# A transformer block in float32: the second half of the tokens is stored by token tiles, two feed-forward blocks change their form, and some transfers are moved

## The chip, the core and the metric

The kernel runs on one core of one Trainium2 chip. A core has five engines that run their own instruction lists side by side: TensorE (PE in the profile; its weight loads are listed apart as PEld) multiplies matrices and writes to PSUM, VectorE (DVE) and ScalarE (ACT) work on tiles in PSUM and SBUF, GpSimd (POOL) works on tiles in SBUF, and SyncE (SP) issues nearly all transfers of this kernel. Transfers (DMA) run on 16 DMA engines. Each engine takes its instructions in the order in which they were written; an instruction that has to wait holds back all that stand behind it on its engine. The metric is the device time in microseconds, from one execution of the whole program; lower is better.

## The reference

One transformer block on 2048 tokens of width 640, all in float32:

```python
q, k, v = qkv[0], qkv[1], qkv[2]                # 32 heads of width 20
scores = jnp.einsum("bhqd,bhkd->bhqk", q, k) * (Dh ** -0.5)
o = jnp.einsum("bhqk,bhkd->bhqd", softmax(scores), v)
h = x + o.transpose(0, 2, 1, 3).reshape(B, S, D) @ wo      # qkv = layernorm(x) @ wqkv
g = silu(layernorm(h) @ w_gate)                 # 640 -> 1728
h2 = h + (g * (layernorm(h) @ w_up)) @ w_down   # 1728 -> 640
```

## The kernel before

**Precision.** Each float32 operand of a product is split into a rounded part "hi" and a remainder "lo" (helper `split`: ACT writes hi, DVE or POOL writes lo, lines L78 and L79), and three matmuls take the place of one (hi·hi, lo·hi, hi·lo).

**The stages.** First come the q, k, v products (up to about 340 us), then attention (to about 1560 us), where each of 32 units is four heads by 512 queries, then the output product and the second layernorm, then the feed-forward part. While attention runs, `prepare_weights` splits the feed-forward weights on POOL, one task in most slots of the loop, and stores them in DRAM: `w_d` for gate and up, `d_d` (one block of rows, plain) and `j_d` (two blocks together) for down.

**The feed-forward part.** The 1728 hidden columns are 14 blocks of 128 (`f` = 0 to 13, the last one half wide). The 2048 tokens are four chunks of 512, taken in two pairs: chunks 0 and 1 ("pair 0"), then chunks 2 and 3 ("pair 1"). The list `ELEMENTS` is pair 0 with f = 13, 0, 1, ..., 12 and then pair 1 with the same, 28 elements `e`. An element's gate and up products for both chunks are done by `blocks` with a scheme of sums that needs 54 matmuls of 512 columns instead of 60; it reads the chunks' normalized, transposed activations `z2_c` and sums of them, `t14` and `t32`, as moving operand, in 8 steps (`products`, L1038, into the four PSUM banks `ps_a`). The weights come through `unit_ring`, `last_ring` (SP issues the loads, L824).

**The down products** follow one step at a time, in between, from the list `waiting` (`next_down`; how many per step says the table `RATES`). Two blocks f, f+1 are normally done together: seven steps for 256 tokens, each of three matmuls of 320 columns (`seven`, L1123, four banks `ps_b`), whose operand `yp` needs sums and splits on POOL and ACT (`prepare`, L1113 to L1116 and L78, L79), and whose results go partly to `h` and partly to sums of their own (`own`), which are added to `h` at the end on POOL (L1161). A block done alone ("plain": before, f = 12 and 13 of pair 0 and f = 10 to 13 of pair 1) takes four steps for 256 tokens and adds to `h` directly on DVE (L1128). The down weights come through `down_ring`, nine places of the tile `halves`.

**The late tokens.** SBUF holds one pair at a time. So during the first elements of pair 0 the chunks 2 and 3 are normalized, transposed on PE (L1374, five matmuls per tile of 128 tokens, two `ps_a` banks), copied by ACT to `zz` (L1379), split to a staging tile `kept` (L78, L79; two buffers), and written to DRAM (`z_d`); POOL forms the sums of the two chunks (L1391), which are split and written as well (`t_d`). The rows of `h` themselves are written too (`h_d`). This work is a list `late` of which one item runs at the end of each step, four items per tile of 128 tokens of both chunks, 17 in all. The writes are put on SP's list one item after the split (`store`, L1347). Down products of two blocks together can only begin when this list is empty, since their tiles `yp` and `own` take its place.

**The swap.** At the end of pair 0 the new activations and sums are loaded over the old ones (`swap`, L1420, at the steps in `SWAPS`), and `h` of chunks 2 and 3 comes back (`bring_back`).

## Time and profile before

| what | value |
|---|---|
| three timed runs, median | 2158.71 us |
| lowest, highest | 2153.14, 2159.97 us |
| the profiled execution's own time | 2154.66 us |
| its span, first to last instruction | 2152.9 us |
| PE busy in the span | 2092.1 us (97%) |
| DVE, ACT, POOL busy | 1739.1, 1302.5, 729.0 us |
| moved by DMA | 294.28 MB, 137 GB/s over the span |

A page of the profile gives busy times by engine, the span in 40 slices, the transfers, the chain of work that ended last, and the costliest groups of instructions. Rows of a timeline are: start in us, duration in us, engine and source line, operation, output<-input, shapes, how many were merged (x), and in brackets how long the engine was idle before and what ended that. "PEclk" is the granted TensorE clock as a share of full speed. The span of a row of merged matmuls reaches a little past the start of the next row, because matmuls overlap; the pitch from one row's start to the next row's start is what they cost. In a stage table the numbers behind an engine are its busy time and its count of instructions.

### The profile page before, as it was taken

The page shows a single profiled execution, that of the slowest core. Times are in us where ns is not written, and L with a number is a line of the kernel's source. Part 1 is how long each engine was busy: PE and PEld are TensorE (multiplying, and loading weights), DVE is VectorE, ACT ScalarE, POOL GpSimd, SP SyncE. Part 2 cuts the span into 40 slices and gives each one's busy share as a digit, 9 for nine tenths or more (in the row PEclk, how much of TensorE's full clock was granted, in tenths as well). Part 3 has the DMA queues.
Part 4 walks back from the last instruction along what each step waited for, and adds up shares of the span by engine and source line. Part 5 has one row for each costly group of instructions (what it writes and reads, how often), then busy time and mean ns, then how long its engine had stood idle before and what let it go on. Part 6 is the DMA issues. An engine that isn't in the chain of part 4 may idle for free.

```text
span 2152.9 us, 35419 instructions
## 1 busy us (share of the span) xinstructions
PE 2092.1 (97%) x12594; PEld 1213.1 (56%) x12594; DVE 1739.1 (81%) x2885; ACT 1302.5 (60%) x2587; POOL 729.0 (34%) x1037
## 2 busy tenths in 40 slices
PE   7999999999999999999999999999996999999999
PEld 5766775333333333333333333345685788788888
DVE  6999997999999999999999999974373566566667
ACT  4322217999989999999999999976632222112221
POOL 5222212343342433443300001011155544565447
PEclk9999999999999999999999999999998999999999
DMA  7665533342524434435412122211259446785452
GB/s 239 180 180 168 155 106 93 113 147 78 169 89 146 129 119 125 158 107 156 142 47 63 48 68 54 73 59 52 64 178 284 146 156 201 284 283 168 162 184 96
DMA packets 213833, 294.28 MB, mean 137 GB/s; under 512 B 46792, under 2 KB 99016, under 8 KB 213656
## 3 DMA queue, kind: packets, MB, share of 16 engines
q1 hardware_dynamic: 200072, 265.79, 39.0%
q10 hardware_dynamic: 13584, 26.23, 4.0%
q8 instruction: 100, 1.64, 0.3%
q14 instruction: 77, 0.63, 0.1%
HBM read 196.77 MB, written 94.37 MB: 135 GB/s over the span
## 4 chain that ended last, share of the span: by engine, by line
PE 85%; DMA 5%; DVE 4%; POOL 3%; ACT 1%; issue 1%; SPq 0%; ACTq 0%; POOLq 0%; DVEq 0%
PE acc L878 23%; PE ps_max L179 15%; PE ps_one L868 14%; PE ps_a L1038 13%; PE ps_b L1123 7%; PE ps_one L420 5%; DVE mx L173 3%; PE ps_wide L169 2%; PE ps_one L454 2%; PE ps_max L611 2%; DMA z_d<-kept 1%; DMA halves<-j_d 1%; PE ps_b L611 1%; DMA t_d<-kept 1%; DMA o_t<-o_d 1%
## 5 line engine op out<-in xcount | busy, mean ns | idle before, releaser
L874 ACT ACTIVATE probs<-ps_one 128x512 f32<-128x512 f32 x2048 | 1045.0, 623 | 134.8 <-PE ps_one L868 130.0
L185 DVE TENSOR_REDUCE mx<-ps_max 128x1 f32<-128x512 f32 x1632 | 1021.0, 683 | 95.5 <-PE ps_max L179 50.5
L868 PE MATMUL ps_one<-q_stk,k_stk 62*128 62x512 f32 x2048 | 550.5, 421 | 3.9 <-ACT probs L874 3.2
L878 PE MATMUL acc<-probs,v_stk 128*32 128x512 f32 x4096 | 546.3, 605 | 0.3
L179 PE MATMUL ps_max<-k_stk,q_stk 60*128 60x512 f32 x1632 | 541.1, 459 | 2.4 <-DVE mx L185 1.5
L179 PEld LDWEIGHTS ps_max<-k_stk,q_stk 60*128 60x128 f32 x1632 | 230.3, 184 | 428.5 <-DVE mx L185 412.5
L868 PEld LDWEIGHTS ps_one<-q_stk,k_stk 62*128 62x128 f32 x2048 | 299.8, 185 | 84.1 <-ACT probs L874 55.1
L173 DVE TENSOR_REDUCE mx<-ps_wide 128x2 f32<-128x1024 f32 x208 | 240.7, 1217 | 14.5 <-PE ps_wide L169 14.1
L1240 DVE TENSOR_TENSOR tmp<-ps_a,tmp 128x512 f32<-128x512 f32 x208 | 141.3, 690 | 136.0 <-PE ps_a L1038 108.7
L1123 PE MATMUL ps_b<-halves,yp 128*128 128x320 f32 x1116 | 197.5, 312 | 15.2 <-ACT yp L78 5.6
L1123 PEld LDWEIGHTS ps_b<-halves,yp 128*128 128x128 f32 x1116 | 180.1, 190 | 35.3 <-issue 7.1
L878 PEld LDWEIGHTS acc<-probs,v_stk 128*32 128x32 f32 x4096 | 80.8, 108 | 159.9 <-issue 151.5
L1038 PE MATMUL ps_a<-t,units 128*128 128x512 f32 x624 | 167.1, 405 | 0.1
L196 POOL CAST both<-neg 128x16 fp32r<-128x16 f32 x32 | 6.6, 206 | 467.3 <-DVE neg L192 228.3
L1038 PE MATMUL ps_a<-z,units 128*128 128x512 f32 x516 | 135.5, 398 | 0.0
L79 POOL TENSOR_TENSOR yp<-y,yp 128x256 fp32r<-128x256 f32 x104 | 65.0, 625 | 198.2 <-ACT yp L78 198.1
L1038 PEld LDWEIGHTS ps_a<-t,units 128*128 128x128 f32 x624 | 115.7, 193 | 20.5 <-DVE kept L79 1.0
L1128 DVE TENSOR_TENSOR h<-ps_b,h 128x320 f32<-128x320 f32 x228 | 103.4, 482 | 8.0 <-PE ps_b L1123 7.0
L1285 ACT ACTIVATE tmp<-tmp 128x512 f32<-128x512 f32 x26 | 16.4, 632 | 147.7 <-DVE tmp L1240 147.6
L1038 PEld LDWEIGHTS ps_a<-z,units 128*128 128x128 f32 x516 | 94.5, 190 | 16.8 <-ACT tmp L1254 0.5
L78 ACT ACTIVATE yp<-tmp 128x512 fp32r<-128x512 f32 x44 | 27.8, 632 | 121.3 <-POOL tmp L1116 121.3
L1038 PE MATMUL ps_a<-z,lasts 128*128 128x512 f32 x324 | 92.7, 394 | 0.7 <-DMA z<-z_d 0.7
(155 smaller groups left out, 2061.6 us busy)
## 6 DMA issues: line engine op xcount, KB each, us to landing
units<-w_d SPq DMA_DIRECT2D x186, 256.0 KB
w_d<-stage SPq DMA_DIRECT2D x106, 256.0 KB
halves<-j_d SPq DMA_DIRECT2D x77, 320.0 KB
j_d<-stage SPq DMA_DIRECT2D x42, 320.0 KB
raw<-qk_d SPq DMA_DIRECT2D x70, 160.0 KB
k_stk<-qk_d SPq DMA_DIRECT2D x64, 160.0 KB
q_stk<-qk_d SPq DMA_DIRECT2D x64, 160.0 KB
rb<-r_d SPq DMA_DIRECT2D x32, 256.0 KB
```

Of the source, the lines that this page charges most:

```text
L79: lo_engine.tensor_tensor(out=lo, in0=src, in1=hi.bitcast(F32), op=ALU.subtract)
L173: nc.vector.tensor_reduce(mx[:, :, pair, t, kc], ps, axis=AX.X, op=ALU.max)
L179: nc.tensor.matmul(ps, queries[u][rows, pair, t * P : (t + 1) * P], keys[u // NC][rows, pair, kc * CH : (kc + 1) * CH], start=True, stop=True,
L185: nc.vector.tensor_reduce(mxs[u][:, b, pair, t, kc : kc + 1], ps, axis=AX.X, op=ALU.max)
L420: nc.tensor.matmul(ps, w[:, k, m * P : (m + 1) * P], a[:, k, :], start=(n == 0 and k == 0), stop=(n == 2 and k == ND - 1),)
L868: nc.tensor.matmul(ps, keys[u // NC][rows, p, kt * P : (kt + 1) * P], queries[u][rows, p, :], start=True, stop=True,)
L874: nc.scalar.activation(probs[p][:, b, :], ps, AF.Exp, scale=scale)
L878: nc.tensor.matmul(acc[32 * j : 32 * j + 32, :], values[u // NC][:, kt, j * VW : j * VW + 32], probs[j // 2][:, j % 2, :], start=(kt == 0) ...
L1038: nc.tensor.matmul(ps, w[k][:, i], z[k][:, j], start=(first and m == 0), stop=(last and m == len(n) - 1),)
L1123: nc.tensor.matmul(ps, a, b, start=(n == 0), stop=(n == len(pairs) - 1))
L1128: nc.vector.tensor_tensor(out=h, in0=ps, in1=h, op=ALU.add)
L1240: add = lambda out, ps, x: nc.vector.tensor_tensor(out=out, in0=ps, in1=x, op=ALU.add)
```

## The change

1. **Layout.** `z_d` and `z2_c`, and `t_d`, `t14`, `t32`, are stored by token tile and part: for each quarter of the columns, first the token tile t, then hi or lo, then the two column blocks, then 128 tokens. A write of one token tile now puts 512 numbers (2 KB) in a row, where it put 128 (512 bytes). The moving operand of an `L1038` product (L1057 now) is now four stretches of 128 numbers, 512 numbers apart, where it was 512 in a row. The loads of the swap take one stretch of a partition instead of two.
2. **Staging.** Three tiles instead of two hold a 512-column split until it is written: one of its own, and two that lie over places 6 to 9 of `halves`, which has ten places now instead of nine. As long as the list of late items isn't empty, `down_ring` issues six loads only.
3. **More, smaller late items.** Six per tile of 128 tokens instead of four (a `store` between the two transposes, the two splits of the sums apart; the lo part of the second goes to DVE): 26 instead of 17, so that the list ends in element 4 at step 4 instead of element 3 at step 3. `h` of chunk 2 is written before, in the loop of the last output products.
4. **Two blocks plain.** f = 0 and 1 of pair 0 are done alone: their y is split when it is formed, and their down products need neither `yp` nor `own`, so that they run while the late items do (`RATES` are raised to 10 to 14 for the elements 1 to 6). `prepare_weights` gets a load and four pieces of weights more (7 tasks).
5. **The swap** loads the sums T2, T1, T3 and T4 in elements 14 and 15, where T2 and T1 were loaded in element 13. Also, in the last attention units, the rows of x for `h` are loaded one slot later, behind the second load of `o_t`.

SP's list at the first late writes. `kept` and `halves` are staging tiles; the shape at the end of a row is how many stretches, then what is in one. Before:

```order
L1347 DMA h_d<-h_19637 128x640
L1347 DMA z_d_63<-kept_20182 256x1x128
L1347 DMA z_d_63<-kept_20185 256x4x128
L824 DMA units<-w_d_68 128x512
L1347 DMA h_d<-h_19636 128x640
L1347 DMA z_d_64<-kept_20217 256x1x128
L1347 DMA z_d_64<-kept_20220 256x4x128
L824 DMA units<-w_d_68 128x512
L824 DMA units<-w_d_69 128x512
L1347 DMA t_d_65<-kept_20265 1024x1x128
```

Now:

```order
L1380 DMA z_d_63<-kept_20224 128x256
L1380 DMA z_d_63<-kept 128x2x512
L843 DMA units<-w_d_68 128x512
L843 DMA units<-w_d_69 128x512
L1380 DMA z_d_64<-kept_20286 128x256
L1380 DMA z_d_64<-halves 128x2x512
L843 DMA lasts<-w_d_70 128x512
L843 DMA units<-w_d_69 128x512
L1380 DMA t_d_65<-halves 256x1x512
L843 DMA units<-w_d_69 128x512
L1380 DMA t_d_66<-kept 256x1x512
```

The writes have longer stretches, one `h_d` write per tile is gone, and more unit loads stand between them.

PE's list from the second transpose of the second token tile (chunk 3) to the next one (chunk 2, third tile). `z`, `t` with `units` or `lasts` are the gate and up products, `halves,y` are down products. Before:

```order
L1374 MATMUL ps_a<-ident,z_20285 128x128 x5
L1038 MATMUL ps_a<-t_19639,units 128x512 x6
L1123 MATMUL ps_b<-halves,y 128x320 x2
L1038 MATMUL ps_a<-z_0_3040,units 128x512 x6
L1038 MATMUL ps_a<-z_0_3040,lasts 128x512 x3
L1123 MATMUL ps_b<-halves,y 128x320 x2
L1038 MATMUL ps_a<-t_19638,units 128x512 x6
L1123 MATMUL ps_b<-halves,y 128x320 x4
L1374 MATMUL ps_a<-ident,z_20319 128x128 x5
```

Now:

```order
L1421 MATMUL ps_a<-ident,z_20372 128x128 x5
L1057 MATMUL ps_a<-t_19656,units 128x512 x6
L1057 MATMUL ps_a<-z_0_3042,lasts 128x512 x3
L1151 MATMUL ps_b<-halves,y 128x320 x6
L1057 MATMUL ps_a<-z_1_3043,units 128x512 x6
L1057 MATMUL ps_a<-z_1_3043,lasts 128x512 x3
L1151 MATMUL ps_b<-halves,y 128x320 x3
L1057 MATMUL ps_a<-z_1_3043,lasts 128x512 x3
L1151 MATMUL ps_b<-halves,y 128x320 x6
L1057 MATMUL ps_a<-z_0_3042,units 128x512 x6
L1151 MATMUL ps_b<-halves,y 128x320 x3
L1421 MATMUL ps_a<-ident,z_20425 128x128 x5
```

Four steps instead of three lie between the two transposes, with 27 matmuls of 512 columns instead of 21 and 18 of 320 columns instead of 8.

SP's list at the swap, from the first load of a new activation on. Before:

```order
L1420 DMA z_0_3040<-z_d_63 128x2x1024
L824 DMA units<-w_d_80 128x512
L1420 DMA t_19639<-t_d_66 128x2x1024
L824 DMA units<-w_d_67 128x512
L824 DMA halves<-j_d_90 128x640
L1420 DMA z_0_3040<-z_d_63 128x2x1024
L824 DMA units<-w_d_67 128x512
L824 DMA halves<-j_d_90 128x640 x2
L1420 DMA t_19638<-t_d_65 128x2x1024
```

Now:

```order
L1468 DMA z_0_3042<-z_d_63 128x2048
L843 DMA units<-w_d_80 128x512
L843 DMA halves<-d_d_85 128x640 x2
L843 DMA units<-w_d_67 128x512
L843 DMA halves<-d_d_86 128x640
L1468 DMA z_0_3042<-z_d_63 128x2048
L843 DMA units<-w_d_67 128x512 x3
L1468 DMA z_0_3042<-z_d_63 128x1024
L843 DMA units<-w_d_67 128x512
L1468 DMA z_1_3043<-z_d_64 128x2048
```

The loads of `t` are gone from between the loads of `z`, and the down weights (`halves`) stand at another place of their own sequence.

The core of the diff:

```diff
-    z_d = [dram.tile([P, 2, ND, CH], F32R, name=f"z_d{c}") for c in range(2)]
-    t_d = [dram.tile([P, 2, 4, CH], F32R, name=f"t_d{i}") for i in range(2)]
+    z_d = [dram.tile([P, 2 * ND * CH], F32R, name=f"z_d{c}") for c in range(2)]
+    t_d = [dram.tile([P, 8 * CH], F32R, name=f"t_d{i}") for i in range(2)]
...
+    def quarter(z, q):
+        z = z[:, q * 4 * CH : (q + 1) * 4 * CH]
+        return z.rearrange("p (t i k n) -> p t i k n", t=TPC, i=2, k=2)
+    def rest_of(z):
+        return z[:, 8 * CH :].rearrange("p (t i n) -> p t i n", t=TPC, i=2)
...
-                    if kt == NT - 4 and c < NC - 1:
+                    if kt == NT - 3 and c < NC - 1:
                         ahead[4]()
...
             nc.tensor.matmul(
-                ps, w[k][:, i], z[k][:, j],
+                ps.rearrange("p (t n) -> p t n", t=TPC), w[k][:, i], z[k][:, :, j],
                 start=(first and m == 0), stop=(last and m == len(n) - 1),
             )
+    def tokens(z, q):
+        return [quarter(z, q)[:, :, :, k] for k in range(2)]
...
     def own(pair, f):
-        return f >= (NF - 2, NF - 4)[pair]
+        return f >= NF - 4 if pair else f < 2 or f >= NF - 2
...
-        by_unit(ps, two_of(z0))
+        by_unit(ps, tokens(z0, 0))
...
+        if i > 3:
+            nc.sync.dma_start(h_d[0, :, i - 4], h_c[2][:, i - 4, :])
     pc_ctx.close()
...
-    halves = pd2.tile([P, 9, 2, HALF], F32R, name="halves")
+    halves = pd2.tile([P, 10, 2, HALF], F32R, name="halves")
...
-    down_ring.fill()
+    down_ring.fill(6)
...
-        def keep(src, dst, lo_src=None, lo_engine=nc.gpsimd):
-            n = src.shape[1]
-            t = pl.tile([P, 2, n, P], F32R, name=f"kept{n}", bufs=2)
-            split(src, t[:, 0], t[:, 1], lo_engine)
-            stores.append((dst.bitcast(F32), t.bitcast(F32)))
+        flat = [pl.tile([P, 2 * CH], F32R, name="kept")] + [
+            halves[:, i : i + 2].rearrange("p a i n -> p (a i n)")[:, : 2 * CH] for i in (6, 8)
+        ]
+        kept = [0]
+        def keep(src, dst, t, lo_engine=nc.gpsimd):
+            f = flat[kept[0] % 3]
+            kept[0] += 1
+            to = f.rearrange("p (q i k n) -> p q i k n", q=2, i=2, k=2)
+            split(src.rearrange("p (q k) n -> p q k n", q=2), to[:, :, 0], to[:, :, 1], lo_engine)
+            dst = dst[:, : 8 * CH].rearrange("p (q t n) -> p q t n", q=2, t=TPC)[:, :, t]
+            stores.append((dst.bitcast(F32), f.rearrange("p (q n) -> p q n", q=2).bitcast(F32)))
...
+        items.append(store)
         for t in range(TPC):
             items.append(lambda t=t: (store(), apply(3, t), flip(2, t)))
+            items.append(store)
             items.append(
                 lambda t=t: (store(), t + 1 < TPC and apply(2, t + 1), flip(3, t))
             )
             items.append(lambda: (store(), sums()))
-            items.append(lambda t=t: (keep_sums(0, t), keep_sums(1, t)))
+            items.append(lambda t=t: (store(), keep(zz[2], t_d[0], t)))
+            items.append(lambda t=t: (store(), keep(zz[3], t_d[1], t, nc.vector)))
...
-    SWAPS = {13: ("B11", "T2", "B21", "T1", "", "K0", "B22", "K1"), 14: ("", "", "T3", "T4")}
+    SWAPS = {
+        13: ("B11", "", "B21", "", "", "K0", "B22", "K1"), 14: ("T2", "", "T1", "", "T3"), 15: ("T4",),
+    }
...
-        1: (6, 2), 2: (10, 0), 3: (4, 7), 4: (17, 0), 14: (12, 0), 15: (16, 0), 16: (16, 0),
+        1: (10, 2), 2: (12, 0), 3: (13, 0), 4: (13, 0), 5: (14, 2), 6: (13, 0),
+        14: (12, 0), 15: (16, 0), 16: (16, 0),
...
+            if (pair, f) in EARLY:
+                ys[i] = tuple(
+                    pd2.tile([P, CH], F32R, name="y", tag="y", bufs=7) for _ in range(2)
+                )
+                split(s, *ys[i], nc.gpsimd)
```

More of the change, by code (lines that the diff above doesn't have):

```diff
@@ L818, in __init__, with fill @@
             self.issued = self.taken = self.freed = self.before = 0
-        def fill(self):
-            while self.issued < min(len(self.plan), self.before + len(self.places)):
+        def fill(self, most=None):
+            most = len(self.plan) if most is None else most
+            while self.issued < min(most, self.before + len(self.places)):
                 place = self.places[self.issued % len(self.places)]
@@ L1234, in plain, with blocks @@
                 step()
-    def blocks(step, done):
+    def blocks(step, done, place):
         u = {"K4": last_ring.take()}
@@ L1242, in mul @@
         def mul(x, y):
-            out = pd2.tile([P, CH], F32, name="y", tag="y", bufs=7)
+            out = place()
             nc.vector.tensor_tensor(out=out, in0=x, in1=y, op=ALU.mult)
@@ L1260, in blocks @@
         ps = bank()
-        by_unit(ps, two_of(z0, 2), True, False)
-        products(ps, one_of(u["K4"], 0), one_of(z0, ND - 1), False)
+        by_unit(ps, tokens(z0, 1), True, False)
+        products(ps, one_of(u["K4"], 0), [rest_of(z0)], False)
         add(p1, ps, p1)
@@ L1275, in blocks @@
         ps = bank()
-        by_unit(ps, two_of(t14, 2), True, False)
-        products(ps, one_of(u["K4"], 1), one_of(z0, ND - 1), False)
+        by_unit(ps, tokens(t14, 1), True, False)
+        products(ps, one_of(u["K4"], 1), [rest_of(z0)], False)
         add(u2, ps, u2)
@@ L1281, in blocks @@
         ps = bank()
-        by_unit(ps, two_of(z1, 2), True, False)
-        products(ps, one_of(u["K4"], 0), one_of(z1, ND - 1), False)
+        by_unit(ps, tokens(z1, 1), True, False)
+        products(ps, one_of(u["K4"], 0), [rest_of(z1)], False)
         add(u5, ps, u5)
@@ L1328, in tile_block @@
         if own(pair, f):
-            plan += [(d_d[f - NF + 4], i) for i in range(2)]
+            plan += [(d_d[f], i) for i in range(2)]
         elif f % 2:
@@ L1332, in tile_block @@
     down_ring = Ring(
-        [halves[:, i] for i in range(9)],
+        [halves[:, i] for i in range(10)],
         [lambda t, d=d, i=i: (t.rearrange("p i n -> p (i n)"), d[:, i]) for d, i in plan],
     )
-    down_ring.fill()
+    down_ring.fill(6)
     pl_ctx = ExitStack()
@@ L1449, in step @@
             at[0] += 1
-            for ring in (unit_ring, last_ring, down_ring):
-                ring.fill()
+            unit_ring.fill()
+            last_ring.fill()
+            down_ring.fill(6 if late else None)
             bring_back()
-            if (e, n) == (3, 4):
+            if (e, n) == (4, 5):
                 assert not late
@@ L1460, in step @@
                 next_down()
-            if not late and e > 2:
-                prepare_some()
+            prepare_some()
             for _ in range(2):
@@ L1496, in tile_block @@
         else:
-            (plain if f == NF - 1 else blocks)(step, done)
+            if f == NF - 1:
+                plain(step, done)
+            else:
+                blocks(step, done, tmp if (pair, f) in EARLY else y_place)
         before = ys
```

111 lines of the change are left out of this document (67 added, 44 removed).

## The prediction

> **What bounds the kernel now.** I read the stages first, then PE's waits in the stage that falls out, then the rows around those waits. In the table of stages PE is the first engine named, then its weight loads, DVE, ACT and POOL; PEclk, DMA share and GB/s end the row.
>
> ```profile
> 340.00:1340.00 1000.00, 999.07 (x6748) 391.80 (x6746) 920.88 (x1518) 910.34 (x1816) 298.29 (x503) 1.00 0.35 106
> 1600.00:1700.00 100.00, 77.73 (x337) 62.91 (x336) 50.05 (x100) 26.98 (x57) 51.09 (x63) 0.86 0.74 238
> 1700.00:1800.00 100.00, 100.00 (x516) 87.03 (x515) 66.26 (x129) 21.58 (x48) 46.94 (x75) 1.00 0.56 182
> 1860.00:1920.00 60.00, 54.36 (x276) 45.87 (x275) 36.40 (x69) 9.55 (x20) 43.03 (x53) 1.00 0.91 328
> 1920.00:2100.00 180.00, 180.00 (x928) 156.73 (x928) 122.68 (x237) 40.02 (x88) 82.20 (x136) 1.00 0.55 182
> ```
>
> PE bounds nearly everything: full in attention, full in the steady feed-forward stages, at clock 1.00. Two stretches fall out. From 1600 to 1700, where the late tokens are written, PE is idle for 100 − 77.73 = 22.3 us and its clock is 0.86. From 1860 to 1920, the swap, it is idle for 5.6 us. PE's waits from 1560 to 1700 (engine and line, who ended the wait; us, times, longest):
>
> ```profile
> PE ps_a L1374 <- ACT zz L1379: 10.4, 3, 4.5
> PE ps_b L1123 <- ACT yp L78: 5.6, 1, 5.6
> PE ps_b L1123 <- POOL yp L79: 2.3, 2, 1.9
> PE ps_a L1374 <- DVE z L1357: 2.0, 2, 1.1
> PE ps_b L1123 <- DVE own L1144: 1.8, 1, 1.8
> ```
>
> The transposes wait for ACT's copies, and the first joint down products for `yp` and `own` once the list is empty. What ACT waits for shows in the chain of waits (start, duration):
>
> ```profile
> 1612.46 6.14 DMA z_d<-kept
> 1618.68 0.64 ACT kept L78
> 1619.39 1.28 POOL kept L79
> 1620.68 3.79 DMA t_d<-kept
> ```
>
> A split (0.64 + 1.28) and then a write that must leave the staging tile before ACT may fill it again: a ring of two tiles, driven by transfers. Four splits per token tile on two buffers are two rounds of about (6.14 + 3.79) / 2 + 1.92 = 6.9 us, so 13.8 us; the rows below show 14.7 from one stall to the next (1619.85, 1634.54). PE has far less to do in that time.
>
> **The slow clock is the second half of the loss.** PE's timeline:
>
> ```profile
> 1619.85 0.48 PE L1374 MATMUL ps_a<-ident,z 128*128 128x128 f32 x1 [4.52 <-ACT zz L1379]
> 1620.34 2.93 PE L1038 MATMUL ps_a<-t,units 128*128 128x512 f32 x6
> ...
> 1628.33 0.71 PE L1374 MATMUL ps_a<-ident,z 128*128 128x128 f32 x5
> 1628.79 1.64 PE L1038 MATMUL ps_a<-t,units 128*128 128x512 f32 x6
> ...
> 1634.54 0.43 PE L1374 MATMUL ps_a<-ident,z 128*128 128x128 f32 x1 [3.38 <-ACT zz L1379]
> 1635.03 2.92 PE L1038 MATMUL ps_a<-t,units 128*128 128x512 f32 x6
> ...
> 1655.63 4.38 PE L1038 MATMUL ps_a<-t,units 128*128 128x512 f32 x18
> 1659.84 0.86 PE L1038 MATMUL ps_a<-z,lasts 128*128 128x512 f32 x3
> ...
> 1682.83 1.04 PE L1123 MATMUL ps_b<-halves,yp 128*128 128x320 f32 x6
> 1683.70 1.55 PE L1038 MATMUL ps_a<-z,units 128*128 128x512 f32 x6
> ```
>
> Six matmuls that take 1.64 us at 1628.79 take 2.93 after a stall. At full clock one of 512 columns costs (1659.84 − 1655.63) / 18 = 0.234 us, one of 320 columns (1683.70 − 1682.83) / 6 = 0.145, five transposes 1628.79 − 1628.33 = 0.46. The groups of PE from 1600 to 1700 (count behind x):
>
> ```profile
> L1038 PE MATMUL ps_a<-t,units 128*128 128x512 f32 x90 | 28.3, 462 | 0.1
> L1038 PE MATMUL ps_a<-z,units 128*128 128x512 f32 x64 | 18.6, 429 | 0.0
> L1123 PE MATMUL ps_b<-halves,yp 128*128 128x320 f32 x63 | 13.9, 363 | 9.7 <-ACT yp L78 5.6 <-POOL yp L79 2.3 <-DVE own L1144 1.8
> L1038 PE MATMUL ps_a<-z,lasts 128*128 128x512 f32 x48 | 13.9, 400 | 0.0
> L1123 PE MATMUL ps_b<-halves,y 128*128 128x320 f32 x32 | 7.2, 319 | 0.0
> L1374 PE MATMUL ps_a<-ident,z 128*128 128x128 f32 x40 | 6.9, 290 | 12.5 <-ACT zz L1379 10.4 <-DVE z L1357 2.0
> ```
>
> At those prices 202 × 0.234 + 95 × 0.145 + 8 × 0.46 = 64.8 us; PE was busy 77.7, so the clock cost 12.9. That stage loses 22.3 + 12.9 = 35.2 us.
>
> **The change part by part.**
>
> *Late stage, PE's side.* The elements 1 to 4 hold 4 × 54 gate and up matmuls (50.5 us), 16 plain steps of two and 32 of three down matmuls (128 × 0.145 = 18.6) and eight transposes (3.7): 72.8 us in 32 steps, 2.28 a step. Six items per token tile instead of four give PE 13.7 us of work per tile, where the old ring alone took 14.7.
>
> *Late stage, the ring's side.* Four splits on three tiles are 4/3 rounds per tile: even at the old transfer times 4/3 × 6.9 = 9.2 us, below 13.7. Longer stretches should shorten it more. The transfers there:
>
> ```profile
> DMA packets 24648, 21.14 MB, mean 302 GB/s; under 512 B 1027, under 2 KB 19459, under 8 KB 24644
> ...
> 1860.00:1880.00 20.00, 15.60 (x77) 12.51 (x76) 10.44 (x20) 2.68 (x6) 10.53 (x14) 1.00 1.04 399
> ```
>
> The first row is 1600 to 1670; 19459 of its 24648 packets are under 2 KB, and it moves 302 GB/s. The second is the swap, with large pieces and full queues: 399. After the change the stage moves by count 5.2 MB (`z_d`), 4.2 (`t_d`), 1.3 (`h_d`), 2.0 (`halves`) and about 7.6 (weights), 20 MB in 29 steps of 2.28 = 66 us, 307 GB/s: three quarters of what the second row reached.
>
> [...]
>
> *What is late next.* DVE. Its work per element, from these rows (busy, mean ns):
>
> ```profile
> L1240 DVE TENSOR_TENSOR tmp<-ps_a,tmp 128x512 f32<-128x512 f32 x208 | 141.3, 690 | 136.0 <-PE ps_a L1038 108.7
> L1128 DVE TENSOR_TENSOR h<-ps_b,h 128x320 f32<-128x320 f32 x228 | 103.4, 482 | 8.0 <-PE ps_b L1123 7.0
> L1357 DVE TENSOR_SCALAR z<-h,mvs,r_late 128x640 f32<-128x640 f32 x8 | 4.9, 618 | 0.0
> ```
>
> Ten adds and products of 0.69, twelve additions to `h` of 0.48, and for 1 1/3 token tiles two normalizations (0.62), two small splits and one lo of 512 columns (together about 1.3, an estimate from 0.69 for 512 columns): 6.9 + 5.8 + 3.4 = 16.1 us against PE's 18.2. It fits, without much room. POOL's new splits of y wait for a freed y tile once (element 2, step 7); behind them stand POOL's later lo parts, whose write has three steps. I leave 4 us idle and 2 us of slow clock, between 0 (PE bound) and the old 35.2. Term: −(35.2 − 6) = **−29.2**.
>
> *First joint products.* They now begin in element 5 at step 2, five steps (11 us) after their first `prepare`, which took 1669 to 1676 before; the 9.7 us of waits on `yp` and `own` are in the 22.3 already. Their seven pieces of 320 KB can be issued only when the list is empty: 2.3 MB, 6 us at 399 GB/s, for 11 us.
>
> *Swap.* PE's waits from 1860 to 1890:
>
> ```profile
> PE ps_b L1123 <- DMA halves<-j_d: 4.2, 3, 2.7
> PE ps_a L1038 <- DMA z<-z_d: 0.7, 1, 0.7
> ```
>
> Two loads of 1 MB leave that place (2.1 MB, 5.3 us at 399 GB/s), as much as the waits. What is queued behind them later are the unit loads, with seven products in hand. Idle 5.6, I leave 1: **−4.6**; bounds 0 and −5.6.
>
> *Two blocks plain.* 2 blocks × 16 steps × 3 = 96 matmuls instead of 4 × 7 × 3 = 84: 12 × 0.145 = **+1.7**, on PE's path. Their 32 additions to `h` replace 28 on DVE; POOL loses four preparations.
>
> *Moving operand in four stretches.* 26 elements × 54 + 2 × 30 = 1464 matmuls by the code's count. No row before shows one. Nearest: both widths, 0.234 and 0.145, give 0.00046 us per column and nothing for a start (0.234 − 512 × 0.000464 is −0.003), so three more starts cost 0; far end: each stretch costs a transpose (0.46 / 5 = 0.092), 4 × 0.092 − 0.234 = +0.134, 196 us. I take the near end, **0**, because the instruction and its columns stay the same.
>
> *Hidden.* Seven tasks of `prepare_weights` (eight POOL operations of 0.87 us, first row below) lie under attention, where POOL is busy 298 of 1000 us; uncovered they cost 7 us. The 13 steps left at the end instead of 19 leave nothing but PE's own work. The h loads move behind the second `o_t` load; PE's only wait there is
>
> ```profile
> L688 POOL TENSOR_TENSOR stage<-raw,stage 128x320 fp32r<-128x320 f32 x26 | 22.6, 871 | 2.1
> ...
> PE ps_one L868 <- ACT probs L874: 3.2, 1, 3.2
> ```
>
> with ACT behind the first `o_t` load, which is ahead of both in either order: 0, between −3.2 and +3.2.
>
> **Sum.** −29.2 − 4.6 + 1.7 = −32.1. Span 2152.9 → 2120.8, the profiled execution 2154.66 → 2122.6. That one lies 4.05 below the median of the runs; on the median it is 2158.71 − 32.1 = 2126.6. I predict **2126 us**.
>
> **Rivals.**
>
> *Half of the late loss stays.* DVE's 16.1 of 18.2 us come in bursts, and ACT, in order, still waits for a staging tile; each of eight transposes then stalls about 1.8 us with its slow clock, 14 us more: 2141. For it: the clock loss comes with stalls as short as 3.38 us. Against: the ring has 4.5 us to spare per tile.
>
> *Transfers no faster.* 20 MB at 302 GB/s are 66 us, PE's own time, so unevenness shows: some 7 us more, 2133. Against: the ring needs 9.2 of 13.7 us even so.
>
> *A new wait eats it.* The seven j_d pieces and the y tiles stall element 5 and 6, and the sums T2, T1, T3, T4, now loaded up to one element before use, stall element 15; 25 us or more: 2152 to 2164. Against: the swap's queue shortens by as many bytes.
>
> *Slower: the stretched operand.* If TensorE pays at each jump, place: every L1038 matmul. 32 / 1464 = 0.022 us each cancels the gain, a tenth of 0.234; at 0.03 it is 2126 + 44 = 2170. For it: no row excludes it. Against: the two widths show no start cost. [...]
>
> **How the numbers follow.** Forecast 2115 to 2137: 0.60. Better, all waits gone and the 1480 to 1500 wait too: below 2115, 0.04. Transfers no faster 0.10, half kept 0.13, eaten 0.07, slower 0.06. The range to 2147 holds the forecast, the transfers' rival and most of the half-kept one: 0.60 + 0.10 + 0.11, so 2115 to 2147. A measurement of this kernel tells about 0.3% (6.5 us) from no change. Faster: 0.60 + 0.04 + 0.10 + 0.13 = 0.87; same 0.07; slower 0.06.
>
> **What would show it.** Right: from the first late write to the first joint product PE is idle under 5 us at clock near 1.00, the transposes' wait on ACT is gone, `kept` no longer makes ACT wait for DMA, the late stage moves about 300 GB/s, L1057's six stay at 1.40 us pitch; at the swap `halves` ends no PE wait above 1 us. Wrong: a pitch above 0.25 us per 512 columns; DVE as what ends PE's waits in elements 2 to 4; a wait on `halves<-j_d` in element 5 or on `t<-t_d` in element 15.

## The result and the profile after

The changed kernel takes 2122.99 us (median of four runs, 2119.72 to 2123.96), the kernel before 2155.93 beside it (four runs, 2151.19 to 2159.97): a ratio of 0.9845, 95% interval 0.9819 to 0.9872. It is faster by 1.5%, inside the range and 3 us below the 2126 forecast; 2.8 of these 3 us come from the base, since the kernel before took 2155.93 in this group and 2158.71 in the one the forecast started from. Its profiled execution took 2123.73 us with a span of 2121.9, so 31.0 us left the span where −32.1 were forecast.

Stages of the changed kernel (PE, PEld, DVE, ACT, POOL busy, then PEclk, DMA share, GB/s). From the swap on its work lies 24 to 31 us earlier than before, so 1831 to 1891 answers to the 1860 to 1920 of before:

```profile
1600.00:1700.00 100.00, 97.19 (x495) 83.45 (x495) 75.50 (x149) 30.27 (x63) 51.20 (x61) 0.98 0.78 273
1620.00:1640.00 20.00, 17.73 (x87) 15.26 (x86) 12.70 (x24) 7.75 (x16) 10.94 (x12) 0.91 0.61 215
1831.00:1891.00 60.00, 58.72 (x307) 51.21 (x306) 40.22 (x77) 10.42 (x21) 42.91 (x53) 1.00 1.00 368
```

In the late stage PE ran 495 matmuls in the time in which it ran 337; its idle time fell from 22.3 to 2.8 us, its clock rose from 0.86 to 0.98. At the swap 1.3 us of idle time are left of 5.6, though the transfers there are no less busy (DMA share 1.00, 0.91 before). PE's groups from 1600 to 1700 give the slow clock, as in the prediction:

```profile
L1057 PE MATMUL ps_a<-t,units 128*128 128x512 f32 x120 | 32.7, 409 | 2.3 <-DVE tmp L1272 2.3
L1057 PE MATMUL ps_a<-z,units 128*128 128x512 f32 x95 | 24.7, 394 | 0.0
L1151 PE MATMUL ps_b<-halves,y 128*128 128x320 f32 x128 | 24.0, 312 | 0.0
L1057 PE MATMUL ps_a<-z,lasts 128*128 128x512 f32 x61 | 17.7, 396 | 0.0
L1151 PE MATMUL ps_b<-halves,yp 128*128 128x320 f32 x51 | 9.1, 312 | 0.5 <-DVE own L1172 0.5
L1421 PE MATMUL ps_a<-ident,z 128*128 128x128 f32 x40 | 6.2, 290 | 0.0
```

276 × 0.234 + 179 × 0.145 + 8 × 0.46 = 94.2 us of work in 97.2 busy: 3.0 us of slow clock, where it was 12.9. The eight transposes wait for nothing now (12.5 us before), the joint products for 0.5 (9.7 before). Of PE's waits from 1440 to the end these matter most:

```profile
PE ps_one L887 <- ACT probs L893: 3.4, 1, 3.4
PE ps_a L1057 <- DVE tmp L1272: 2.3, 1, 2.3
...
PE ps_b L1151 <- POOL yp L81: 1.3, 1, 1.3
```

The first is the end of attention, unchanged (3.2 before). The second is all that is left in the late stage beside 0.5 us for `own`. The third is the one wait left at the swap. PE's timeline there, then DVE's, ACT's and POOL's:

```profile
1621.38 0.74 PE L1151 MATMUL ps_b<-halves,y 128*128 128x320 f32 x4
1624.39 2.10 PE L1057 MATMUL ps_a<-t,units 128*128 128x512 f32 x6 [2.27 <-DVE tmp L1272]
1626.29 1.00 PE L1151 MATMUL ps_b<-halves,y 128*128 128x320 f32 x3
```

```profile
1617.79 0.88 DVE L1156 TENSOR_TENSOR h<-ps_b,h 128x320 f32<-128x320 f32 x2
1622.45 1.28 DVE L81 TENSOR_TENSOR kept<-zz,kept 128x512 fp32r<-128x512 f32 x1 [3.79 <-issue]
1623.66 0.68 DVE L1272 TENSOR_TENSOR tmp<-ps_a,tmp 128x512 f32<-128x512 f32 x1
```

```profile
1621.21 0.63 ACT L80 ACTIVATE halves<-zz 128x512 fp32r<-128x512 f32 x1 [4.07 <-POOL zz L1438]
1621.75 0.61 ACT L80 ACTIVATE kept<-zz 128x512 fp32r<-128x512 f32 x1
```

```profile
1616.74 1.30 POOL L81 TENSOR_TENSOR y<-tmp,y 128x512 fp32r<-128x512 f32 x1 [1.29 <-ACT y L80]
1618.01 3.18 POOL L1438 TENSOR_TENSOR zz<-zz 128x256 f32<-128x256 f32 x4
```

Read from the bottom: POOL does a lo part of y first and ends the sums of the chunks at 1621.2; ACT writes their hi parts at 1621.2 and 1621.8; DVE's lo part of the second sum, at the head of its queue, can only run at 1622.45, after 3.79 us in which DVE did nothing; the product's evaluation (`tmp`, L1272) stands behind it, and PE waits 2.27 us for the bank. The six matmuls after it take 1.90 us from their start to the next row's, where six take 1.40 at full clock.

### The profile page after: what moved, and what is told of

Its sections match the earlier page's. It is cut to its first block, busy times and chain, and to the rows that moved or that the text cites. A ratio compares the mean times of both kernels' runs of the same rounds, so it can differ in the third digit from the quotient of the medians.

```text
span 2121.9 us, 35575 instructions
## 1 busy us (share of the span) xinstructions
PE 2081.7 (98%) x12606; PEld 1208.7 (57%) x12606; DVE 1748.7 (82%) x2893; ACT 1300.4 (61%) x2579; POOL 716.5 (34%) x1017
## 4 chain that ended last, share of the span: by engine, by line
PE 87%; DVE 5%; DMA 4%; POOL 1%; issue 1%; ACT 1%; SPq 0%; ACTq 0%; DVEq 0%; POOLq 0%
PE acc L897 24%; PE ps_max L181 15%; PE ps_one L887 15%; PE ps_a L1057 14%; PE ps_b L1151 8%; PE ps_one L422 4%; DVE mx L175 3%; PE ps_one L456 2%; PE ps_wide L171 2%; PE ps_max L625 2%; PE ps_b L625 1%; DMA raw<-qk_d 1%; DVE mx L187 1%; DMA o_t<-o_d 0%; DMA xt<-in_A_x 0%
## 5 line engine op out<-in xcount | busy, mean ns | idle before, releaser
L887 PE MATMUL ps_one<-q_stk,k_stk 62*128 62x512 f32 x2048 | 550.5, 421 | 4.1 <-ACT probs L893 3.4
L887 PEld LDWEIGHTS ps_one<-q_stk,k_stk 62*128 62x128 f32 x2048 | 299.8, 185 | 84.4 <-ACT probs L893 55.2
L1272 DVE TENSOR_TENSOR tmp<-ps_a,tmp 128x512 f32<-128x512 f32 x208 | 141.3, 690 | 118.2 <-PE ps_a L1057 92.5
L1151 PE MATMUL ps_b<-halves,yp 128*128 128x320 f32 x1032 | 179.3, 308 | 2.0 <-POOL yp L81 1.3
L1151 PEld LDWEIGHTS ps_b<-halves,yp 128*128 128x128 f32 x1032 | 165.1, 188 | 18.6 <-POOL yp L81 1.5
L1057 PE MATMUL ps_a<-t,units 128*128 128x512 f32 x624 | 163.7, 398 | 2.3 <-DVE tmp L1272 2.3
L1057 PE MATMUL ps_a<-z,units 128*128 128x512 f32 x516 | 133.6, 393 | 0.0
L1057 PEld LDWEIGHTS ps_a<-t,units 128*128 128x128 f32 x624 | 113.0, 189 | 21.4 <-DVE tmp L1272 2.5
L81 POOL TENSOR_TENSOR yp<-y,yp 128x256 fp32r<-128x256 f32 x96 | 60.4, 630 | 188.1 <-ACT yp L80 180.1
L1156 DVE TENSOR_TENSOR h<-ps_b,h 128x320 f32<-128x320 f32 x248 | 110.0, 481 | 6.9 <-PE ps_b L1151 5.2
L1057 PEld LDWEIGHTS ps_a<-z,units 128*128 128x128 f32 x516 | 93.2, 187 | 16.0
L265 ACT ACTIVATE e<-ps_one 128x512 f32<-128x512 f32 x37 | 22.1, 598 | 115.8 <-PE ps_one L422 76.2
L1057 PE MATMUL ps_a<-z,lasts 128*128 128x512 f32 x324 | 92.6, 393 | 0.0
```

Source lines behind the costliest of these rows:

```text
L887: nc.tensor.matmul(ps, keys[u // NC][rows, p, kt * P : (kt + 1) * P], queries[u][rows, p, :], start=True, stop=True,)
L1057: nc.tensor.matmul(ps.rearrange("p (t n) -> p t n", t=TPC), w[k][:, i], z[k][:, :, j], start=(first and m == 0), stop=(last and m == len(n ...
L1151: nc.tensor.matmul(ps, a, b, start=(n == 0), stop=(n == len(pairs) - 1))
L1156: nc.vector.tensor_tensor(out=h, in0=ps, in1=h, op=ALU.add)
L1272: add = lambda out, ps, x: nc.vector.tensor_tensor(out=out, in0=ps, in1=x, op=ALU.add)
```

## The experiments

The theory was the prediction's: the ring of staging tiles against the work that PE has per token tile set the old stalls (**pace and ring**), and the swap's wait went because two 1 MB loads left its place. Rivals: one part alone did it (the longer pieces, the third tile, the plain blocks), or DVE alone made the stall.

**The change once more.** The same kernel, without an edit, as the reference beside the next three.

> The changed kernel once more, as the measure for the others of this set. Both theories: 2120 to 2124 us, with the one stall of 2.3 us in the first token tile, where a matmul into ps_a waits for DVE.

2121.49 us (2119.93 to 2124.34) against 2153.84: 0.9847 (0.9822 to 0.9872). The gain is there again, and so is the stall of 2.27 us, but this time without a slow clock behind it:

```profile
1621.97 1.67 PE L1057 MATMUL ps_a<-t,units 128*128 128x512 f32 x6 [2.27 <-DVE tmp L1272]
1623.48 0.60 PE L1151 MATMUL ps_b<-halves,y 128*128 128x320 f32 x3
```

The six matmuls take 1.51 us, and the granted clock is 1.00 from 1600 to 1700. So the slow clock behind this stall comes in one execution of the kernel (1.90 us for the six) and not in another (1.51).

**Short pieces.** The writes of a split go out in stretches of 512 bytes again, in two stores.

```diff
-            to = f.rearrange("p (q i k n) -> p q i k n", q=2, i=2, k=2)
+            to = f.rearrange("p (i k q n) -> p q i k n", q=2, i=2, k=2)
...
-            stores.append((dst..., f.rearrange("p (q n) -> p q n", q=2)...))
+            f = f.rearrange("p (b q n) -> p q b n", q=2, b=4)
+            for q in range(2):
+                stores.append((dst[:, q].bitcast(F32), f[:, q].bitcast(F32)))
```

> Only the order of the staging tile is changed, so that a late write goes out in pieces of 512 bytes again, as two transfers of 256 KB instead of one of 512 KB; DRAM, the swap and all else stay. Theory A (pace: PE now has about 13.7 us of its own work per token tile, more than the ring of staging tiles needs): the ring at the old transfer times is 4/3 x 6.9 = 9.2 us, so nothing on PE, 2120 to 2127 us. Theory B (the longer pieces removed the waits): at the old 302 GB/s the stage's 20 MB take 66 us, as long as PE, the transposes wait for ACT again and ACT for the writes: 2130 us or more.

2122.22 us; 0.9847 (0.9815 to 0.9879): no difference. The transfers from 1600 to 1670, of the changed kernel and of this one:

```profile
DMA packets 10954, 19.92 MB, mean 285 GB/s; under 512 B 1004, under 2 KB 2028, under 8 KB 10949
```

```profile
DMA packets 22644, 19.71 MB, mean 282 GB/s; under 512 B 1232, under 2 KB 17664, under 8 KB 22639
```

The stretches are short again (17664 packets under 2 KB), the bytes per time the same. The stage's row of this kernel:

```profile
1600.00:1700.00 100.00, 96.76 (x494) 83.12 (x493) 74.66 (x149) 30.36 (x63) 51.28 (x61) 0.98 0.84 272
```

The DMA share is 0.84 against 0.78 for the same 272 to 273 GB/s. So short stretches cost the DMA engines some time, which nobody waited for: divided by the share of time in which the engines were busy, the rate is 272 / 0.84 = 324 GB/s, with the long ones 273 / 0.78 = 350. In the kernel's time they cost nothing that can be told (0.9847 both times). The 302 against 399 GB/s that the prediction set side by side is no measure of the pieces: the stage with long ones moves only 285, and its engines are not full (DMA share 0.81 over the same 1600 to 1670).

**Two staging tiles.** The third is not used.

```diff
-            f = flat[kept[0] % 3]
+            f = flat[1 + kept[0] % 2]
```

> Only two staging tiles are used, as before the change. Theory A (pace): two rounds per token tile at the old transfer times are 13.8 us against 13.7 of PE work, and the pieces are longer now, so at most 2 us of new idle time: 2121 to 2127 us. Theory C (the third tile removed the waits): half of the old stalls are back, 8 to 15 us: 2131 to 2138 us, with ACT waiting for DMA of its staging tile.

2124.62 us (2111.86 to 2125.0); 0.9846 (0.981 to 0.9882): no difference.

**Four items per token tile.** The two `store` items go and the two splits of the sums are one item again, 17 in all.

```diff
-        items.append(store)
...
-            items.append(store)
...
-            items.append(lambda t=t: (store(), keep(zz[2], t_d[0], t)))
-            items.append(lambda t=t: (store(), keep(zz[3], t_d[1], t, nc.vector)))
+            items.append(lambda t=t: (keep(zz[2], t_d[0], t), keep(zz[3], t_d[1], t, nc.vector)))
```

> The late list is merged back to four items per token tile, 17 in all; plain blocks, third tile and longer pieces stay. Theory A (pace): PE's own work per token tile falls to 4 x 2.28 = 9.1 us, and the stage's transfers would have to run at 20 MB in 46 us = 435 GB/s, above the 399 seen so far, so PE stalls at the transposes, 4 to 12 us with the slow clock: 2127 to 2135 us. Theories B and C (ring): 4/3 rounds of a shorter write still fit, no change: 2120 to 2126 us.

2133.59 us (2130.5 to 2138.33); 0.9904 (0.9877 to 0.9931): slower than the change by 12 us, but what it waits for is not what the ring would make it wait for. PE's wait, then DVE's timeline in it:

```profile
PE ps_a L1421 <- DVE z L1404: 13.2, 4, 6.6
```

```profile
1615.57 1.28 DVE L81 TENSOR_TENSOR kept<-zz,kept 128x512 fp32r<-128x512 f32 x1 [4.06 <-issue]
```

The lo part on DVE again, nearer to the normalization behind it. The run mixes the pace with DVE's held queue and decides nothing on the ring; the last three of the late stage below are without that part.

**The first two blocks joint again.** Blocks 0 and 1 of pair 0 are done together, with a table of rates for that.

```diff
-        return f >= NF - 4 if pair else f < 2 or f >= NF - 2
+        return f >= NF - 4 if pair else f >= NF - 2
...
-                if self.fs[0] == (2, 0)[self.pair]:
+                if self.fs[0] == 0:
...
-        1: (10, 2), 2: (12, 0), 3: (13, 0), 4: (13, 0), 5: (14, 2), 6: (13, 0),
+        1: (6, 2), 2: (10, 0), 3: (0, 0), 4: (6, 6), 5: (22, 0), 6: (20, 0), 7: (18, 0), 8: (16, 0),
...
-    EARLY = ((0, 0), (0, 1))
+    EARLY = ()
```

> The blocks 0 and 1 of pair 0 are done together again, after the late list is empty; their steps are made up in elements 4 to 8 (6, 22, 20, 18, 16 steps). Layout, three tiles and 26 items stay. 12 matmuls of 320 columns fewer, -1.7 us. Theory A (pace): PE's own work per token tile falls from 13.7 to about 11.2 us, still above the ring's 9.2, but the transfers go to 20 MB in 54 us = 370 GB/s: 0 to 6 us of stalls, 2120 to 2127 us. If the plain blocks are what removed the waits: 10 us or more, 2133 us or above.

2126.91 us (2121.69 to 2132.96) against 2156.94; 0.9861 (0.984 to 0.9882). PE's groups from 1600 to 1700:

```profile
L1151 PE MATMUL ps_b<-halves,yp 128*128 128x320 f32 x93 | 18.6, 345 | 6.8 <-DMA halves<-j_d 4.5 <-POOL yp L81 2.3
...
L1421 PE MATMUL ps_a<-ident,z 128*128 128x128 f32 x40 | 6.2, 290 | 0.0
```

The transposes still wait for nothing. The first joint products wait again, 6.8 us where it was 9.7, but most of it is a new wait: 4.5 us for their weights, where the old one was for ACT's `yp` (5.6) and for `own` (1.8). Only POOL's 2.3 us are as they were. The weights come late because the six loads of `halves<-j_d` are issued at 1659.52, behind the last late write: the change lets `down_ring` issue six loads only until the late list is empty, and the table of rates of this run starts the joint products right after that. So the run shows that the transposes don't need the plain blocks; it doesn't show by itself that the plain blocks took the old 9.7 us away. Its time can't be told from the change's (the intervals overlap).

**The old table of the swap.**

```diff
-        13: ("B11", "", "B21", "", "", "K0", "B22", "K1"), 14: ("T2", "", "T1", "", "T3"), 15: ("T4",),
+        13: ("B11", "T2", "B21", "T1", "", "K0", "B22", "K1"), 14: ("", "", "T3", "T4"),
```

> Only the table of swap steps is put back: the sums T2 and T1 are loaded in element 13 again, T3 and T4 in element 14. Theory A: 2.1 MB stand before the activations and down weights again, and PE waits 4 to 5 us for halves or z: 2126 to 2129 us. Rival: the tenth place of halves and loads in one stretch cover it, no change: 2120 to 2125 us.

2123.0 us (2118.81 to 2126.47); 0.9841 (0.9822 to 0.986): nothing is lost. Its only wait on a load at the swap:

```profile
PE ps_a L1057 <- DMA z<-z_d: 2.0, 2, 1.0
```

There is no wait on `halves`, with T2 and T1 back in element 13. Moving them was not what took the 4.2 us away.

**The lo part of the second sum on POOL.**

```diff
-            items.append(lambda t=t: (store(), keep(zz[3], t_d[1], t, nc.vector)))
+            items.append(lambda t=t: (store(), keep(zz[3], t_d[1], t)))
```

> Only the lo part of the second sum goes back from DVE to POOL. Theory A: the stall of 2.3 us in the first token tile is DVE held by this one instruction, which waits for ACT, which waits for POOL's sums; without it the stall and the slow clock behind it go, 3 to 4 us: about 2119 us, and PE's row with the wait for DVE is gone. Rival: POOL gets 1.3 us more per token tile, the write is put on the queue later and the wait comes back elsewhere: 2122 to 2126 us.

2119.48 us (2113.12 to 2124.75, five runs); 0.9822 (0.98 to 0.9845). The wait for DVE's `tmp` is gone from the late stage:

```profile
1600.00:1700.00 100.00, 98.95 (x512) 84.90 (x511) 75.22 (x147) 31.02 (x64) 56.67 (x65) 1.00 0.81 278
```

512 matmuls in these 100 us instead of 495 (502 in the second profile of the changed kernel, also at clock 1.00). The stall was this one instruction's place rather than DVE's load: DVE did nothing for 3.79 us ahead of it, and it is busy for as long in these 100 us without it (75.2 against 75.5 us). In the kernel's time the 2 to 3 us can't be told from none; the intervals overlap.

**The same, and an `o_t` split later.** For chunk 2 the last entry of `ahead[0]`, ACT's work on `o_t` in attention's last slots, runs one slot later.

```diff
-                if NT - 4 <= kt < NT - 1:
-                    ahead[0][kt - NT + 4]()
+                late_part = c == 2 and kt >= NT - 2
+                if NT - 4 <= kt < NT - 1 and not late_part or late_part and kt == NT - 1:
+                    ahead[0][min(kt - NT + 4, 2)]()
```

> As the one before, and in attention's last unit but one ACT's first split of o_t is put one slot (about 2.4 us) later, so that ACT's exponentials don't stand behind a transfer that has not landed. Theory A: ACT's wait of 3.5 us falls to about 1, PE's of 3.4 to about 1, and with it most of the slow clock from 1493 to 1505: 3 to 6 us on top, about 2114 us. Rival: PE waits for the split's lo part instead, no gain over the one before.

2117.9 us (2112.09 to 2119.59); 0.9814 (0.9796 to 0.9831). PE's wait for ACT's `probs` is no longer in its list, whose only other entry above 1 us, beside attention's own 1.3, is now

```profile
PE ps_b L1152 <- DMA halves<-j_d: 1.2, 1, 1.2
```

but the median moved by 1.6 us only, which cannot be told from none. This is the lowest median of the study, 39 us below the kernel before in its own group.

**Four items, lo on POOL.** The edit of the four items, with `keep(zz[3], t_d[1], t)` in place of `nc.vector`: the pace alone, with the new ring.

```diff
+            items.append(lambda t=t: (keep(zz[2], t_d[0], t), keep(zz[3], t_d[1], t)))
```

> Four items per token tile again, as in e3, but the second sum's lo part on POOL (in e3 the waits of 13.2 us on DVE came from this part on DVE, not from a transfer). Plain blocks, third tile and 2 KB pieces stay. If e3 lost by DVE alone: no stall, as e6, 2117 to 2122 us. Theory A (pace): 9.1 us of PE work per token tile and 20 MB in about 46 us, 435 GB/s against 399 seen, so 5 us of stalls with ACT waiting for DMA of the staging tiles, and slow clock: 2123 to 2129 us.

2126.51 us (2123.95 to 2136.24) against 2153.02; 0.9884 (0.9859 to 0.991): in the range of theory A. The transposes' group, which holds all the stage's idle time but 0.5 us, and ACT's timeline at the longest of these waits:

```profile
L1421 PE MATMUL ps_a<-ident,z 128*128 128x128 f32 x40 | 6.4, 278 | 6.6 <-ACT zz L1426 4.4 <-DVE z L1404 2.2
```

```profile
1640.48 1.15 ACT L80 ACTIVATE halves<-zz 128x512 fp32r<-128x512 f32 x2 [3.80 <-POOL zz L1438]
...
1642.06 0.57 ACT L1426 ACTIVATE zz<-ps_a 128x512 f32<-128x512 f32 x1
```

The reason is not theory A's. ACT's copy of the transposes (L1426) stands behind the hi parts of the sums, and these wait for POOL's sums (L1438), 3.80 us here and 3.28 and 3.06 us at the other two waits, not for a transfer. With four items the next transposes come two items after the sums, with six they come three after.

**Six items with the old ring whole.** Two tiles, 512-byte stretches, lo on POOL: the edits of the short pieces, of the two tiles and of the lo part together.

```diff
+            f = flat[1 + kept[0] % 2]
...
+            to = f.rearrange("p (i k q n) -> p q i k n", q=2, i=2, k=2)
```

> As e6 (six items, lo on POOL), with the old ring whole: two staging tiles and pieces of 512 bytes. Theory A (pace): the old ring's 13.8 us per token tile against 13.7 of PE work, so 0 to 4 us over e6: 2118 to 2124 us. Theory of the ring: half of the old stalls come back, 2130 us or more.

2122.86 us (2114.13 to 2129.17); 0.9855 (0.9821 to 0.9888). ACT's waits from 1590 to 1680, where the two staging tiles bear the name `halves`, and then PE's from 1440 on:

```profile
ACT halves L80 <- DMA t_d<-halves: 9.5, 5, 3.4
ACT halves L80 <- DMA z_d<-halves: 4.3, 2, 2.3
```

```profile
PE ps_a L1057 <- ACT tmp L1285: 2.2, 1, 2.2
```

ACT stands 13.8 us for a staging tile again (22.7 before the change, 1.5 with the new ring and the lo part on POOL), and the transposes do not wait at all; one product does, for 2.2 us (0.6 with the new ring). ACT's copy before that product stands behind hi parts that wait for POOL's sums. They come 15.3 us after those of the token tile before (1623.78, 1639.04), with the new ring 13.7 us (1622.05, 1635.70); in between, ACT waited 3.40 and 1.23 us for a staging tile, and POOL's lo parts waited for ACT. So the staging tiles have a part in this wait. The time, 3.4 us above the run with the new ring, can't be told from it (0.9855 and 0.9822, with intervals that overlap).

**Four items with the old ring.** Both edits.

```diff
+            f = flat[1 + kept[0] % 2]
...
+            items.append(lambda t=t: (keep(zz[2], t_d[0], t), keep(zz[3], t_d[1], t)))
```

> As e8 (four items, lo on POOL), with the old ring whole: two staging tiles and pieces of 512 bytes; the plain blocks stay. Theory A (pace): 13.8 to 14.7 us per token tile against 9.1 of PE work, four tiles: 19 to 22 us idle and about 10 of slow clock, less what the down products cover: 2140 to 2152 us, with ACT waiting for z_d and t_d. If the plain blocks alone removed the waits: 2119 to 2124 us.

2131.86 us (2128.93 to 2134.13); 0.99 (0.9885 to 0.9915): 5 us above the one with four items and the new ring, with intervals that overlap, and 8 us short of what the theory wanted at least. PE's groups from 1600 to 1700 that wait, and the joint products':

```profile
L1057 PE MATMUL ps_a<-z,units 128*128 128x512 f32 x80 | 21.8, 407 | 3.5 <-ACT tmp L1285 3.5
L1423 PE MATMUL ps_a<-ident,z 128*128 128x128 f32 x40 | 6.4, 278 | 5.9 <-ACT zz L1428 3.5 <-DVE z L1406 2.5
L1151 PE MATMUL ps_b<-halves,yp 128*128 128x320 f32 x33 | 5.6, 308 | 0.0
```

The transposes wait 5.9 us where they waited 12.5, and the joint products not at all. What the new ring spares is the first row, 3.5 us in two waits. ACT's timeline at the longer one:

```profile
1622.43 0.63 ACT L80 ACTIVATE halves<-zz 128x512 fp32r<-128x512 f32 x1 [3.65 <-DMA t_d<-halves]
1622.96 0.58 ACT L1285 ACTIVATE tmp<-ps_a 128x512 f32<-128x512 f32 x1
```

ACT stands 3.65 us for a staging tile, its copy `tmp` stands behind, and PE waits for that copy. My expectation had forgotten that of the old 22.3 us 9.7 were the joint products', which wait for other things than a staging tile, and that the plain blocks' products (128 on `y` in this stage instead of 32) fill time between two stalls; that they cover the rest of the difference is argued, not shown.

**The old table and nine places.** Is it the tenth place, then?

```diff
-        [halves[:, i] for i in range(10)],
+        [halves[:, i] for i in range(9)],
```

> The old table of swap steps, as in e5, and only nine places of halves in the ring. If the tenth place is what took the waits at the swap: PE waits 3 to 5 us for halves there, 2126 to 2129 us. If not (the ring's contents stand differently at the swap, since blocks 0 and 1 are plain, or the loads in one stretch are quicker): under 3 us of waits, 2120 to 2125 us.

(with the edit of the old table). 2125.07 us (2123.08 to 2129.06); 0.9872 (0.9856 to 0.9887). PE's waits from 1840 to 1930:

```profile
PE ps_a L1057 <- DMA z<-z_d: 1.3, 2, 1.0
PE ps_b L1151 <- DMA halves<-j_d: 0.2, 1, 0.2
```

The old wait does not return with the old table and the old number of places. What differs is when the pieces are asked for. SP's timeline of the kernel before, from its last-unit load on, and then of this one:

```profile
1847.81 0.32 SPq L824 DMA_DIRECT2D lasts<-w_d  x1
1850.07 0.57 SPq L1420 DMA_DIRECT2D z<-z_d  x1
...
1853.13 0.42 SPq L824 DMA_DIRECT2D halves<-j_d  x1
...
1855.42 1.50 SPq L824 DMA_DIRECT2D halves<-j_d  x2
...
1861.53 1.13 SPq L824 DMA_DIRECT2D halves<-j_d  x2
```

```profile
1828.51 0.90 SPq L843 DMA_DIRECT2D halves<-j_d  x2
1830.40 0.32 SPq L843 DMA_DIRECT2D lasts<-w_d  x1
1830.76 0.91 SPq L843 DMA_DIRECT2D halves<-j_d  x2
...
1833.51 0.65 SPq L843 DMA_DIRECT2D halves<-j_d  x1
```

Counted from `lasts`, the five pieces stood 5.3 to 13.7 us behind it, after the first loads of activations and sums; now two are ahead of it, two 0.4 us and one 3.1 us behind. Why places come free earlier there was not tried by itself; that it is the plain blocks, which shift the whole list of down products, is only argued, and the run of the joint blocks, which kept ten places and the new table, does not tell. The loads of the swap in one stretch of a partition, which every run kept, are a rival that no run tests.

## Why the prediction was right

**Late stage, −29.2.** Right in size: 35.2 us of loss became 2.8 idle + 3.0 slow clock (4 + 2 were left), −29.4; in the second profile of the same kernel it is 3.3 idle at clock 1.00. Its working was right only in part, and the loss has to be split in two.

The transposes' 12.5 us: with six items they are gone with the plain blocks or without (6.2 us busy and 0.0 idle in the run of the joint blocks) and with the old ring whole; with four items 6 us are left on either ring, 6.6 and 5.9. So it is the number of items. The prediction's reason for it, a ring driven by transfers against PE's work, fits the kernel before, where ACT waited 2.77 and 2.71 us for a staging tile ahead of the copy that ended the transposes' longest wait (4.52 us); with four items on the new ring it is POOL's sums that hold ACT. "The ring's side" was of small weight, not of none: with the old ring ACT's wait for a staging tile reaches PE in 3.5 us at four items, and has a part in 2.2 us at six, at products and not at the transposes. A third tile alone, long stretches alone, and both together change no time that can be told. Six items with the old ring and without the plain blocks were not run.

The joint products' 9.7 us: they are gone in every run with the plain blocks (0.5 us at most is left), even with four items and the old ring. Without them 6.8 us of waits stand there, but 4.5 of these are for weights, which that run's own table makes late. The prediction put the 9.7 us "in the 22.3 already" and named a later start, five steps after the first `prepare`. Whether that start or the plain products themselves removed them stays open.

**What is late next: DVE.** Right, but as a queue rather than as a load. 16.1 of 18.2 us per element did fit; one lo part, waiting at the head for ACT and POOL, held DVE 3.79 us. A sign under "Wrong" in the prediction ("DVE as what ends PE's waits in elements 2 to 4") did come, once, at 2.3 us, inside the 4 us left for it.

**Swap, −4.6.** Right in size: 5.6 us became 1.3. Wrong in its reason: the step "Two loads of 1 MB leave that place, as much as the waits" failed. With both back nothing is lost, and without the tenth place neither, so the number was luck; what took the waits away stays open. The 1.3 us left are one wait, put down to POOL's `yp` in this profile and to `halves<-j_d` in the second one of the same kernel, where the sign "`halves` ends no PE wait above 1 us" fails by 0.3.

**Two blocks plain, +1.7.** Not to be seen by itself: without the plain blocks the kernel does these 12 matmuls less and is not faster, with 6.8 us of waits at the joint products.

**Moving operand in four stretches, 0.** Right. Rows of the changed kernel in the late stage:

```profile
1645.55 1.56 PE L1057 MATMUL ps_a<-t,units 128*128 128x512 f32 x6
1646.95 1.04 PE L1151 MATMUL ps_b<-halves,y 128*128 128x320 f32 x6
```

Six in 1.40 us, 0.233 each, where one was 0.234. The rival with the stretched operand falls, and so does its far end of 196 us; the runs show it for stretches of 512 bytes and for no others.

**Hidden parts, 0.** The wait at the end of attention is 3.2 us before and 3.4 after, for ACT's `probs` both times. In the second profile of the changed kernel it is 1.7 us and put down to a load of `h`; the other runs lie between 1.8 and 3.7, but for the one with the later `o_t` split, where it is gone. So the moved `h` loads gain or lose nothing that can be told. The 7 tasks of preparation and the steps at the end show no wait.

**The sum.** −29.4 − 4.3 + 1.7 = −32.0 against −31.0 measured. The last 1.0 lies ahead of the change: attention's first product (L868, L887 now) starts at 337.77 us before and at 339.10 after, in a part that the change leaves alone. Between the medians the difference is −32.9.

**The other rivals.** "Half of the late loss stays" did not come: one stall of 2.3 us instead of eight of 1.8. "Transfers no faster" was half true: the stage moved 285 GB/s, less than the 302 of before, and PE did not wait. Nor did "a new wait eats it": no wait on `halves<-j_d` in element 5 and none on `t<-t_d` in element 15.

## What to carry to other kernels

Before you rebuild a ring of buffers, count the work that the bounding engine has per round: six list items instead of four took the transposes' stall away with the old ring still making ACT wait 13.8 us, of which PE saw 2.2. Split an idle sum by the group that waits before you give it one cause, follow each wait back to what its releaser itself waited for (with four items the same row, PE waiting for ACT's copy, was mostly the staging tiles before the change and POOL's sums after it), and undo the parts in pairs as well as alone: only with four items does the old ring's 3.5 us show beside the transposes' wait. And a split or copy that depends on two other engines belongs on the engine on which nothing urgent stands behind it; moving one lo part from DVE to POOL took away a stall of 2.3 us.

## What was not expected of the hardware

The clock can fall after stalls shorter than the 3.38 us of the prediction. After 2.27 us without work the next six matmuls of 512 columns took 1.90 us instead of 1.40, and from 1620 to 1640 the granted clock was 0.91. In the run with four items and the old ring a stall of 2.19 us did the same (1.98 us for the six, 0.91 from 1620 to 1640):

```profile
1623.59 2.19 PE L1057 MATMUL ps_a<-z,units 128*128 128x512 f32 x6 [2.19 <-ACT tmp L1285]
1625.57 1.49 PE L1057 MATMUL ps_a<-z,lasts 128*128 128x512 f32 x3
```

But the length of the stall does not settle it. The second execution of the changed kernel, shown above, has the same 2.27 us and no fall (1.51 us for the six, clock 1.00 from 1600 to 1700), and the run with the old table of the swap has 2.2 us and clock 1.00 there too. With four items and the lo part on POOL the longest stall, 2.0 us, came with a clock of 0.91 from 1640 to 1660; with the old ring one of 2.04 us, in the same 20 us, did not (clock 1.00, 1.51 us for the next six). Of the eleven stalls between 2.0 and 2.3 us in the late stages of all profiles, eight came with a fall of the clock (seven in profiles with 0.98 from 1600 to 1700, the one of the joint blocks with 0.91 from 1640 to 1660) and three did not. So the runs give no threshold, and what decides beside the length stays open.
